# Folded weights of four batches made at once on two row halves of TensorE, kept in DRAM

## Chip, cores and metric

The kernel runs on one core of one Trainium2 chip. The metric is device time in microseconds of one execution, taken as the median of several runs. The engines are named as in the profile: PE is TensorE (PEld its weight loads), DVE is VectorE, ACT is ScalarE, POOL is GpSimd, SP is SyncE. SP and POOL issue nearly all DMAs here, each from a queue of its own that is worked off in order.

## What is computed

Memory attention followed by a two-layer network without biases, all in float32:

```python
a   = softmax(phi, over the 576 tokens)          # phi: 8 batches, 8 heads, 576 tokens, 32 memories
k_m = einsum('bhsm,bhsd->bhmd', a, k)            # 32 x 64 for each batch and head
v_m = einsum('bhsm,bhsd->bhmd', a, v)
attn = softmax(q @ k_m.T / 8)                    # 576 x 32
x   = (attn @ v_m), heads side by side           # 4608 tokens x 512
out = relu(x @ w_in)**2 @ w_out                  # w_in 512 x 2048, w_out 2048 x 512
```

The kernel never forms x. It folds v_m into w_in: for each batch, VW = v_m @ w_in (for each head 32 x 64 times 64 x 2048), so that x @ w_in = attn @ VW. This folding is what the change is about.

## The kernel before

**Numbers.** Full precision is kept by splitting each operand into a high part that the fast float32r matmul takes exactly and a low part, and by three products: high*high, high*low, low*high.

**Stages.** The 8 batches are worked off one after the other (0 and 1 interleaved by halves). For each batch there are 16 steps, one for each 128 columns of w_in. A step has `mm1` (line 822): 12 matmuls, attention weights times folded weights, 6 for 256 tokens and 6 for 320, then on ACT and DVE relu, square and the split into `gh` and `glo`; and `mm2` (line 857): 12 matmuls of 512 columns that add to four accumulator banks. `mm2_left` (line 891) does the last 64 tokens of two batches together, 48 matmuls.

**What feeds a batch.** `memory(b, hh)` (line 481) makes k_m and v_m for four heads: a maximum over tokens (`mx`), exp, a sum (`asum`), then 20 float32 matmuls (line 526) that use the array as four column strips of 32, so that four heads are worked side by side; then `kT` for the scores and, through `values` (line 591), the stationary operand `VT` of the folding. `attention(b)` (line 793) makes the attention weights. `vw_step(n, s, hh)` (line 632) does the folding for a pair of batches, 2n and 2n+1: one slice s of 256 columns and one half hh of the chunks. It has 6 matmuls of 256 columns with a block-diagonal stationary operand (128 rows are two heads of 64, the columns are two heads of two batches, and half of the entries are zero), then for each half of the partitions one copy on ACT (line 340, called from 647) and one subtraction on DVE (line 648). A pair takes 16 such steps, and before each, `wi_again` (line 448) loads 512 KB of the prepared w_in from a DRAM copy, `w_in_kept`.

**Buffers.** `V0` to `V7` hold the folded weights of the second batch of a pair, `vw0` (two buffers) those of the first. `mx` is one buffer, used for `mx` and `asum` in turn. `KV` is one buffer, `wi` has three. In PSUM there are four banks `acc`, two banks `h`, one bank `pv` (folding) and one bank `pa` (memory and scores).

**Order.** Nothing is scheduled by hand. `Plan` (line 57) takes all operations with estimated costs, simulates a list schedule forward, then backward (from which due times follow), tries several leads for the operations marked `lead`, and keeps the order whose modelled end is earliest. The order for each engine is fixed in the program; engines meet by semaphores. The last pairs of the program:

```python
    for n in range(1, NPAIR):
        ...
        for b in (b0, b1):
            for hh in (0, 1):
                memory(b, hh)
        attention(b0)
        for s in range(NSL):
            vw_alloc(n, s)
            for hh in (0, 1):
                wi_again(n, s, hh)
                vw_step(n, s, hh)
        ...
        attention(b1)
```

Of the kernel before, what the change touches and what calls it, by code (L numbers as in the profile page):

```python
# [19 lines left out]
P = 128  # L20
# [36 lines left out]
class Plan:  # L57
# [59 lines left out]
    def order(self):  # L117
        for o in reversed(self.ops):
            e = next(iter(o.ways))
            cost = min(o.ways.values()) + (SEES[e] if o.lat is None else o.lat)  # L120
            if o.size:
                cost += sum(n / r for n, r in o.size) + FIRST[e] + LANDS[e] + 300
            late = min((u.late for u in o.users), default=1e9)
            if o.cap is not None:
                late = min(late, o.cap)
            o.late = late - cost
        keys = [o.late - (LEAD if o.lead else 0) for o in self.ops]
        best = self.forward(keys), keys
# [12 lines left out]
        return out  # L141
# [8 lines left out]
    def forward(self, keys):  # L150
# [27 lines left out]
        while left:  # L178
# [35 lines left out]
            for u in o.users:  # L214
                u.count -= 1
                u.ready = max(u.ready, o.end + self.slack(o, u, e))
                if not u.count:
                    add(u)
        return max(o.end for o in self.ops)

    def backward(self):
# [17 lines left out]
        for _ in self.ops:  # L239
# [18 lines left out]
            for x in o.deps:  # L258
                x.ready = max(x.ready, t + self.slack(x, o, x.left) + (0 if x.size else self.seen(x, x.left)))
# [27 lines left out]
def tile_attention_moe(  # L287
# [92 lines left out]
    kept = dram.tile([NSL * 2 * P, 4 * SL], F32, name="w_in_kept")  # L380
    w_kept = plan.buf("w_in_kept", lambda _: kept)
    wi = {}
    wo = {}
# [78 lines left out]
    def vt_alloc(n):  # L462
        for i in (0, 1) if n == 0 else (1 - n % 2,):
            t = [st([P, 4, P], F32R, f"VT{x}{i}", f"VT{x}{n}{i}") for x in "hl"]
            if n:
                VT[2 * n] = VT[2 * n + 1] = t
                continue
# [13 lines left out]
    def memory(b, hh, where=None):  # L481
# [32 lines left out]
        pk = bank(f"pkv{u}")  # L514
        rot = 2 * (b % 2)

# [16 lines left out]
        def sums(e):  # L533
            if asum is None:
                for c in range(SC):
                    r = P if c < NMAIN else LEFT
                    for s in range(4):
                        nc.tensor.matmul(pk()[32 * s:32 * s + 32, 2 * D:2 * D + 1], a()[0:r, (s + rot) % 4, c, :], ones[0:r],
                                         start=(c == 0), stop=(c == SC - 1), tile_position=(0, 32 * s))
            elif b % 2 == 0:  # L540
                nc.tensor.matmul(pk()[:, 2 * D:2 * D + 1], asum(), ones, start=True, stop=True)
# [6 lines left out]
        if b < 2:  # L548
            for i in (0, 1):
                op({"PE": 800}, lambda e, i=i: mm(e, i), [A, KV[i], (pk, "sum")], [(pk, i)], lead=True, lat=120)  # L550
        else:
            op({"PE": 1400}, lambda e: mm(e, 0), [A, KV[0], KV[1], (pk, "sum")], [(pk, 0), (pk, 1)], lead=True, lat=120)
        rs = st([P, 1], F32, "rs", f"rs{u}")
# [4 lines left out]
        if b < 2:  # L558
# [32 lines left out]
    def values(b, hh, pv, at):  # L591
        vh, vl = VT[b]
        for s in (0, 1):
            ch = 2 * hh + ((s + b) % 2)
# [17 lines left out]
    def vw_alone(s, bp):  # L612
# [11 lines left out]
        for hh in (0, 1):  # L624
            op({"PE": 712}, lambda e, hh=hh: mm(e, hh), [ts_[hh], vh, vl], [pw], lead=True)
        V = VW[bp, s]
# [5 lines left out]
    def vw_step(n, s, hh):  # L632
# [8 lines left out]

        op({"PE": 712}, mm, [t, vh, vl], [pw], lead=True)
        for hf in (0, 1):
# [6 lines left out]


    att = {}

    def scores(b, hh, split):

        u = f"{b}_{hh}"
        Q = st([P, NC * D], F32, "q", f"q{u}")
        for x in (0, 1):
            h0 = 4 * hh + 2 * ((x + b) % 2)
            dma(lambda d, x=x, h0=h0: d(Q()[64 * x:64 * x + 64], q[b, h0:h0 + 2].rearrange("h (p c) d -> (h p) (c d)", c=NC)),  # L660
# [333 lines left out]
    for g in range(24, 32):  # L994
        step(g)
    for n in range(1, NPAIR):
        b0, b1 = 2 * n, 2 * n + 1
        vt_alloc(n)
        for b in (b0, b1):
            for hh in (0, 1):  # L1000
                memory(b, hh)
        attention(b0)
        for s in range(NSL):
            vw_alloc(n, s)
            for hh in (0, 1):
                wi_again(n, s, hh)
                vw_step(n, s, hh)
            for ff in (2 * s, 2 * s + 1):
                step(pos[b0, ff])
        attention(b1)  # L1010
        for ff in range(NFF):
            step(pos[b1, ff])

# [33 lines left out]
```

## Time and profile before

| | |
|---|---|
| median of 3 runs | 774.26 us (772.9 to 774.47) |
| the profiled execution, its own time | 774.0 us |
| its span, first to last instruction | 772.1 us |
| PE busy | 749.8 us (97%) |
| DVE busy | 562.0 us (73%) |
| ACT busy | 364.6 us (47%) |
| DMA | 101.54 MB, mean 132 GB/s |

A busy time is the union of the spans of an engine's instructions. Matmuls are pipelined: one of 512 columns is shown with some 400 ns, yet the next one starts 230 ns later. What a matmul costs is therefore read from start to start in the timeline, not from its duration.

### The profile page before, as it was taken

To read this page: it belongs to the slowest core of one execution; us is meant where nothing else is said; L and a number is where in the kernel's file an instruction comes from. 1 tells how busy PE (TensorE), PEld (TensorE's weight loads), DVE (VectorE), ACT (ScalarE), POOL (GpSimd) and SP (SyncE) were. 2 spreads that over 40 slices of the span, in tenths; PEclk is the share of its full clock that TensorE was granted. 3 is DMA by queue.
4 is the path that set the end of the run, shared out by engine and by line. 5 is a ranking of instruction groups with operands and counts; after the bars stand their busy time and mean duration, and the time that the engine had idled before them with its cause. 6 is when DMAs were issued, how large, how long until landed. Compare 5 with 4: busy or idle time off the path is not lost.

```text
span 772.1 us, 13135 instructions
## 1 busy us (share of the span) xinstructions
PE 749.8 (97%) x4998; PEld 646.3 (84%) x4998; DVE 562.0 (73%) x1164; ACT 364.6 (47%) x782; POOL 54.5 (7%) x95
## 2 busy tenths in 40 slices
PE   5889999999999999999999999999999999999997
PEld 3667888888888888888788888888888888888886
DVE  4999999997579655758779567966779566874451
ACT  2767689775443555442333444433335344532330
POOL 4111212111000000010001100010000100000000
PEclk9999999999999999999999999999999999999999
DMA  9998878578556332223545434222334432100002
GB/s 275 338 273 226 263 248 229 172 229 232 155 145 210 102 101 91 59 56 85 147 109 156 134 105 123 81 56 68 93 87 128 129 115 85 31 25 31 1 1 68
DMA packets 70046, 101.54 MB, mean 132 GB/s; under 512 B 21792, under 2 KB 48416, under 8 KB 69984
## 3 DMA queue, kind: packets, MB, share of 16 engines
q1 hardware_dynamic: 59392, 81.41, 35.7%
q0 software_dynamic: 10496, 19.17, 9.3%
q8 instruction: 39, 0.64, 0.4%
q10 hardware_dynamic: 96, 0.13, 0.1%
q14 instruction: 23, 0.19, 0.1%
HBM read 79.17 MB, written 17.83 MB: 126 GB/s over the span
## 4 chain that ended last, share of the span: by engine, by line
PE 83%; DVE 10%; ACT 3%; issue 2%; DMA 1%; SPq 0%; DVEq 0%; ACTq 0%
PE h L843 23%; PE acc L876 14%; PE acc L873 14%; PE acc L874 14%; PE accl L899 6%; PE pvw L640 5%; PE psc L677 3%; PE pkv L526 3%; DVE work L409 1%; DVE work L424 1%; DVE mx L504 1%; DVE vw L648 1%; DVE work L406 1%; DVE wi L439 1%; DVE glo L853 1%
## 5 line engine op out<-in xcount | busy, mean ns | idle before, releaser
L843 PE MATMUL h<-ath,vw 128*128 128x320 f32 (+1 forms) x1024 | 208.1, 298 | 0.2 <-ACT r L847 0.2
L873 PE MATMUL acc<-wo,gh 128*128 128x512 f32 x512 | 206.6, 403 | 0.0
L874 PE MATMUL acc<-wo,gh 128*128 128x512 f32 x512 | 201.9, 394 | 0.0
L843 PEld LDWEIGHTS h<-ath,vw 128*128 128x128 f32 x1024 | 170.7, 189 | 14.3 <-ACT r L847 0.6
L876 PE MATMUL acc<-wo,glo 128*128 128x512 f32 x512 | 158.8, 404 | 0.0
L849 ACT ACTIVATE gh<-r 128x512 fp32r<-128x512 f32 x128 | 81.0, 633 | 110.3 <-DVE r L848 106.3
L340 ACT CAST vw<-pvw 64x512 fp32r<-64x512 f32 (+1 forms) x128 | 74.4, 581 | 99.8 <-PE pvw L640 70.3
L873 PEld LDWEIGHTS acc<-wo,gh 128*128 128x128 f32 x512 | 96.7, 189 | 18.2 <-issue 0.4
L843 PE MATMUL h<-atl,vw 128*128 128x256 f32 (+1 forms) x512 | 110.0, 296 | 0.9 <-DVE atl L778 0.5
L874 PEld LDWEIGHTS acc<-wo,gh 128*128 128x128 f32 x512 | 96.7, 189 | 16.3
L876 PEld LDWEIGHTS acc<-wo,glo 128*128 128x128 f32 x512 | 92.0, 189 | 17.4 <-issue 1.6
L648 DVE TENSOR_TENSOR vw<-pvw,vw 64x512 fp32r<-64x512 f32 x112 | 77.1, 688 | 38.3 <-ACT vw L340 36.5
L853 DVE TENSOR_TENSOR glo<-r,gh 128x512 fp32r<-128x512 f32 x128 | 87.7, 685 | 8.7 <-ACT r L851 5.9
L847 ACT ACTIVATE r<-h 128x256 f32<-128x256 f32 (+1 forms) x151 | 60.6, 411 | 69.6 <-PE h L843 66.8
L848 DVE TENSOR_SCALAR r<-h 128x320 f32<-128x320 f32 (+1 forms) x105 | 47.9, 456 | 56.2 <-PE h L843 55.1
L843 PEld LDWEIGHTS h<-atl,vw 128*128 128x128 f32 x512 | 82.5, 189 | 1.4 <-DVE atl L778 0.7
L852 DVE TENSOR_TENSOR r<-r 128x576 f32<-128x576 f32 x59 | 44.7, 758 | 30.7 <-ACT gl L850 28.2
L899 PE MATMUL accl<-wo,gl 128*128 128x512 f32 x192 | 53.8, 396 | 0.0
L851 ACT ACTIVATE r<-r 128x576 f32<-128x576 f32 x69 | 47.3, 685 | 1.8
L640 PE MATMUL pvw<-wi,VTh 128*128 128x256 f32 x224 | 42.4, 282 | 1.2 <-DVE vw L648 1.2
L640 PEld LDWEIGHTS pvw<-wi,VTh 128*128 128x128 f32 x224 | 37.2, 188 | 6.1 <-issue 1.9
L899 PEld LDWEIGHTS accl<-wo,gl 128*128 128x128 f32 x192 | 34.8, 188 | 6.8
(143 smaller groups left out, 799.6 us busy)
## 6 DMA issues: line engine op xcount, KB each, us to landing
wi<-w_in_kept SPq DMA_DIRECT2D x56, 512.0 KB
KV<-in_v_dram SPq DMA_DIRECT2D x16, 512.0 KB
KV<-in_k_dram SPq DMA_DIRECT2D x16, 512.0 KB
raw<-in_moe_w_in_dram SPq DMA_DIRECT2D x16, 512.0 KB
raw<-in_moe_w_out_dram SPq DMA_DIRECT2D x16, 512.0 KB
w_in_kept<-wi POOLq DMA_DIRECT2D x16, 512.0 KB, 4.6
q<-in_q_dram SPq DMA_DIRECT2D x24, 288.0 KB
out_dram<-o POOLq DMA_DIRECT2D x20, 256.0 KB, 7.8
```

What stands on the lines that cost most here:

```text
L340: nc.scalar.copy(o, i) if e == "ACT" else ENG[e].tensor_copy(o, i)
L640: nc.tensor.matmul(pw()[:, x * SL:(x + 1) * SL], l()[:, 2 * x + hh, :], t()[:, r, x, :], start=(i == 0), stop=(i == 2))
L648: vec({"DVE": 700}, lambda e, part=part, pr=pr: nc.vector.tensor_sub(part(1), pw()[pr], part(0).bitcast(F32)), [pw, (V, (0, hf))], [(V, (1 ...
L843: nc.tensor.matmul(p()[:, 0:n], V()[:, l, hh, c0:c0 + P], x()[:, hh, cs], start=(i == 0), stop=(i == 5))
L847: op({"ACT": act(n) - 40, **({} if b < 2 else {"DVE": tt(n)})}, lambda e, cs=cs, n=n, p=p: nc.scalar.activation(r()[:, cs], p()[:, 0:n], A ...
L848: else nc.vector.tensor_scalar(r()[:, cs], p()[:, 0:n], 0.0, None, ALU.max), [p], [(r, h)])
L849: op({"ACT": act(SM)}, lambda e: nc.scalar.activation(gh(), r()[:, 0:SM], AF.Square), [r], [gh])
L853: vec({"DVE": tt(SM)}, lambda e: nc.vector.tensor_sub(glo(), r()[:, 0:SM], gh().bitcast(F32)), [r, gh], [glo])
L873: nc.tensor.matmul(a(), gh()[:, c], t()[:, 0], start=f0, stop=False)
L874: nc.tensor.matmul(a(), gh()[:, c], t()[:, 1], start=False, stop=False)
L876: nc.tensor.matmul(a(), glo()[:, c], t()[:, 0], start=False, stop=f1)
L899: nc.tensor.matmul(a(), G()[:, l, :], t()[:, w], start=(ff == 0 and n == 0), stop=(ff == NFF - 1 and n == 2))
```

## The change

**Four batches at once.** For batches 4 to 7 `vw_step` is replaced by `vw_quad(s, hh)`. The 128 rows of a w_in chunk are two heads of 64. The stationary operand now holds for the rows of one head the 32 memories of all four batches as 128 columns, with no zeros. Each former matmul over 128 rows becomes two over 64 rows, on the upper and the lower half of the array, into two PSUM banks (`pv` and `pa`). There are 16 such steps of 12 matmuls instead of 32 steps of 6.

**Through DRAM.** The result (a head's slice for four batches on 128 partitions) is split in a tile `fold` (in the room of `KV`), stored to a DRAM tensor by POOL (two stores of 512 KB for each step) and loaded by slice and batch with four DMAs of 128 KB each on SP (`vw_again`) into `V0` to `V7`.

**Order of the program.** All four batches need their v_m first, so `memory` of batches 4 to 7 moves into the steps of batch 2. The k_m of batches 5 to 7 (`kT`) is made in the buffer `mx`, stored to DRAM by POOL and loaded again by SP ahead of the scores. The folding steps stand among the steps of batches 3 and 4: `WHEN` is (2, 5, 8, 11, 14) and (1, 4, 7), and `quad(s)` is `wi_again` and `vw_quad` for both hh. Batches 5 and 7 use the form of the sums that even batches have (line 541, in place of 544).

**Planner.** It takes two matmul operations that follow each other on PE as free of latency, counts 730 for `vw_step` (was 712), 1560 for the memory matmuls (was 1400), 900 for `vw_quad`, and makes more trials.

```diff
-        for _ in range(2):
+        for _ in range(4):
...
-            for lead in (0, 3000, 9000):
+            for lead in (0, 1500, 3000, 6000, 9000):
...
-                u.ready = max(u.ready, o.end + self.slack(o, u, e))
+                u.ready = max(u.ready, t + d if e == "PE" and "PE" in u.ways else o.end + self.slack(o, u, e))
...
+    folded = dram.tile([NSL * 4 * P, 4 * SL], F32, name="vw_kept")
+    w_folded = plan.buf("vw_kept", lambda _: folded)
+    keys = dram.tile([6 * P, 2 * M], F32, name="kT_kept")
+    QUAD = B - 4
...
-        kT = kTs[b, hh] = st([P, 2, 1, M], F32, f"kT{b % 2}{hh}", f"kT{u}")
+        kT = st([P, 2, 1, M], F32, f"kT{b % 2}{hh}" if b <= QUAD else "mx", f"kT{u}")
...
+        if b <= QUAD:
+            kTs[b, hh] = kT
+        else:
+            at = 2 * (b - QUAD - 1) + hh
+            dma(lambda d: d(keys[at * P:(at + 1) * P], kT().rearrange("p u o m -> p (u o m)")), [(2 * M * P * 4, 256)],
+                r=[kT], w=[(w_keys, at)], eng="POOL", lead=True)
...
+    def vw_quad(s, hh):
...
+        Z = room[0]
+        t = wi[QUAD // 2, s, 1, hh]
+        vh, vl = VT[QUAD]
+        pw = [pt(x, f"pvq{s}_{hh}_{x}") for x in ("pv", "pa")]
...
+            for x in (0, 1):
+                for i, (l, r) in enumerate(((vh, 0), (vh, 1), (vl, 0))):
+                    for g in (0, 1):
+                        rows = slice(64 * g, 64 * g + 64)
+                        nc.tensor.matmul(pw[g]()[:, x * SL:(x + 1) * SL], l()[rows, 2 * x + hh, :], t()[rows, r, x, :],
+                                         start=(i == 0), stop=(i == 2), tile_position=(64 * g, 0))
+        op({"PE": 900}, mm, [t, vh, vl], pw, lead=True)
+        for g in (0, 1):
+            part = lambda l, g=g: Z()[:, g, l].rearrange("p x f -> p (x f)")
+            op({"ACT": acp(2 * SL)}, lambda e, part=part, g=g: copy(e, part(0), pw[g]()), [pw[g]], [(Z, (g, 0))], lead=True)
+            vec({"DVE": tt(2 * SL)}, lambda e, part=part, g=g: nc.vector.tensor_sub(part(1), pw[g](), part(0).bitcast(F32)),
+                [pw[g], (Z, (g, 0))], [(Z, (g, 1))], lead=True)
+            at = 4 * s + 2 * hh + g
+            dma(lambda d, g=g, at=at: d(w_folded()[at * P:(at + 1) * P, :], Z()[:, g].rearrange("p l x f -> p (l x f)").bitcast(F32)), [(4096 * P, 4096)],
+                r=[(Z, (g, 0)), (Z, (g, 1))], w=[(w_folded, at)], eng="POOL", lead=True)
...
+    def vw_again(b, s):
+        V = VW[b, s] = st([P, 2, 2, SL], F32R, f"V{s}", f"vw{b}_{s}")
+        for h in range(4):
+            at = (4 * s + h) * P + 32 * (b - QUAD)
+            dma(lambda d, h=h, at=at: d(V()[32 * h:32 * h + 32].rearrange("p l x f -> p (l x f)").bitcast(F32), w_folded()[at:at + 32, :]), [(4096 * 32, 4096)],
+                issue=440, r=[(w_folded, 4 * s + h)], w=[(V, h)], lead=True)
...
+    for s in range(NSL):
+        vw_alloc(1, s)
+        for hh in (0, 1):
+            wi_again(1, s, hh)
+            vw_step(1, s, hh)
+        for ff in (2 * s, 2 * s + 1):
+            step(pos[2, ff])
+        if s == 0:
+            vt_alloc(2)
+        if s == 3:
+            attention(3)
+        memory(QUAD + s // 2, s % 2)
+    for ff in range(NFF):
+        step(pos[3, ff])
+        if ff in WHEN[0]:
+            quad(WHEN[0].index(ff))
+        if ff == 9:
+            attention(4)
+    for b in range(QUAD, B):
+        for ff in range(NFF):
+            if ff % 2 == 0:
+                vw_again(b, ff // 2)
+            step(pos[b, ff])
+            if b == QUAD and ff in WHEN[1]:
+                quad(len(WHEN[0]) + WHEN[1].index(ff))
+            if ff == 9 and b + 1 < B:
+                attention(b + 1)
```

## Rows read from the trace of the kernel before

**Rows 1.** The windows view: PE, PEld, DVE, ACT and POOL busy us with their instruction counts, the granted clock, the DMA share and GB/s; first the stretches of the start, then from 180 us those of the batches (243 is the start of batch 2, then 3, 4, 5, 6, 7; 757 is the tail).

```profile
20.00:60.00 40.00, 34.71 (x411) 27.16 (x410) 37.38 (x88) 27.46 (x57) 5.15 (x10) 0.96 1.03 300
...
140.00:180.00 40.00, 38.81 (x222) 33.58 (x221) 37.18 (x73) 29.53 (x62) 5.34 (x8) 1.00 0.75 219
...
243.00:326.00 83.00, 83.00 (x476) 73.70 (x475) 55.88 (x109) 42.92 (x89) 1.63 (x3) 1.00 0.34 104
326.00:422.00 96.00, 95.28 (x652) 80.98 (x651) 70.48 (x153) 35.05 (x79) 4.97 (x10) 1.00 0.42 106
422.00:508.00 86.00, 86.00 (x490) 76.12 (x489) 61.88 (x123) 38.01 (x78) 2.70 (x4) 1.00 0.34 105
508.00:598.00 90.00, 90.00 (x630) 76.79 (x629) 66.91 (x144) 34.95 (x79) 4.57 (x9) 1.00 0.36 92
598.00:686.00 88.00, 88.00 (x498) 77.82 (x497) 61.54 (x120) 39.29 (x82) 2.58 (x4) 1.00 0.26 79
686.00:757.00 71.00, 71.00 (x392) 62.67 (x391) 35.91 (x70) 19.97 (x49) 0.00 (x0) 1.00 0.05 16
```

**Rows 2.** The timeline of PE around one folding step (start us, us, engine, line, tiles, shape, count).

```profile
480.22 0.40 PE L640 MATMUL pvw<-wi,VTh 128*128 128x256 f32 x2
...
480.57 0.40 PE L640 MATMUL pvw<-wi,VTh 128*128 128x256 f32 x2
...
480.93 0.39 PE L873 MATMUL acc<-wo,gh 128*128 128x512 f32 x1
481.16 0.39 PE L874 MATMUL acc<-wo,gh 128*128 128x512 f32 x1
```

**Rows 3.** The groups by line and form: the folding of the pairs on PE, ACT and DVE (busy us, mean ns of one, idle before).

```profile
L640 PE MATMUL pvw<-wi,VTh 128*128 128x256 f32 x224 | 42.4, 282 | 1.2 <-DVE vw L648 1.2
L340 ACT CAST vw<-pvw 64x512 fp32r<-64x512 f32 x112 | 65.0, 580 | 97.2 <-PE pvw L640 70.3 <-PE h L843 25.4 <-DVE vw L648 0.5
L648 DVE TENSOR_TENSOR vw<-pvw,vw 64x512 fp32r<-64x512 f32 x112 | 77.1, 688 | 38.3 <-ACT vw L340 36.5
L853 DVE TENSOR_TENSOR glo<-r,gh 128x512 fp32r<-128x512 f32 x128 | 87.7, 685 | 8.7 <-ACT r L851 5.9
```

**Rows 4.** The timeline of PE around the memory matmuls on column strips (L526, a row merges 40) and the sums of an even batch (L541).

```profile
543.45 0.39 PE L874 MATMUL acc<-wo,gh 128*128 128x512 f32 x1
543.68 0.28 PE L541 MATMUL pkv<-ones,asum 128*128 128x1 f32 x2
543.82 0.48 PE L873 MATMUL acc<-wo,gh 128*128 128x512 f32 x1
544.13 0.40 PE L874 MATMUL acc<-wo,gh 128*128 128x512 f32 x1
544.46 1.43 PE L526 MATMUL pkv<-KV,phi 128*32 128x128 f32 x40
545.82 0.50 PE L873 MATMUL acc<-wo,gh 128*128 128x512 f32 x1
546.15 0.40 PE L874 MATMUL acc<-wo,gh 128*128 128x512 f32 x1
```

**Rows 5.** From the chain of work that ended last: four full-array float32 matmuls of 320 columns (psc), and the strip matmuls.

```profile
567.29 1.36 PE pkv L526 x40
...
576.00 1.08 PE psc L677 x4
```

**Rows 6.** The timeline of PEld (weight loads) around the same place.

```profile
543.79 0.19 PEld L873 LDWEIGHTS acc<-wo,gh 128*128 128x128 f32 x1
543.90 0.19 PEld L874 LDWEIGHTS acc<-wo,gh 128*128 128x128 f32 x1
```

**Rows 7.** The timeline of PE around the sums of an odd batch (L544).

```profile
555.23 0.40 PE L874 MATMUL acc<-wo,gh 128*128 128x512 f32 x1
555.56 0.28 PE L544 MATMUL pkv<-ones,asum 128*64 128x1 f32 x4
555.77 0.50 PE L876 MATMUL acc<-wo,glo 128*128 128x512 f32 x1
556.20 0.65 PE L526 MATMUL pkv<-KV,phi 128*32 128x128 f32 x16
```

**Rows 8.** The timeline of DVE: two units of `memory` among the steps.

```profile
532.03 1.33 DVE L504 TENSOR_REDUCE mx<-phi 128x128 f32<-128x640 f32 x1
...
539.96 0.81 DVE L510 TENSOR_TENSOR phi<-phi,pmx 128x640 f32<-128x640 f32 x1
...
541.93 1.34 DVE L531 TENSOR_REDUCE asum<-phi 128x128 f32<-128x640 f32 x1 [0.42 <-ACT phi L512]
...
544.17 1.33 DVE L504 TENSOR_REDUCE mx<-phi 128x128 f32<-128x640 f32 x1
...
546.53 0.24 DVE L582 STREAM_TRANSPOSE kT<-kvn 128x64 f32<-128x64 f32 x1
```

**Rows 9.** DMA issues: queue, count, KB each, and where shown the median us from issue to landing.

```profile
w_in_kept<-wi POOLq DMA_DIRECT2D x16, 512.0 KB, 4.6
...
out_dram<-ol POOLq DMA_DIRECT2D x6, 128.0 KB, 6.7
```

**Rows 10.** The timeline of SP's queue: two issues one behind the other (start us, us).

```profile
535.43 0.61 SPq L459 DMA_DIRECT2D KV<-in_v_dram  x1
536.08 0.62 SPq L460 DMA_DIRECT2D KV<-in_v_dram  x1
```

More of the change, by code (lines that the diff above doesn't have):

```diff
@@ L258, in backward @@
             for x in o.deps:
-                x.ready = max(x.ready, t + self.slack(x, o, x.left) + (0 if x.size else self.seen(x, x.left)))
+                x.ready = max(x.ready, t if x.left == o.left == "PE" else t + self.slack(x, o, x.left) + (0 if x.size else self.seen(x, x.left)))
                 x.count -= 1
@@ L381, in tile_attention_moe @@
     w_kept = plan.buf("w_in_kept", lambda _: kept)
+    folded = dram.tile([NSL * 4 * P, 4 * SL], F32, name="vw_kept")
+    w_folded = plan.buf("vw_kept", lambda _: folded)
+    keys = dram.tile([6 * P, 2 * M], F32, name="kT_kept")
+    w_keys = plan.buf("kT_kept", lambda _: keys)
+    QUAD = B - 4
     wi = {}
@@ L465, in vt_alloc @@
             if n:
-                VT[2 * n] = VT[2 * n + 1] = t
+                for b in range(2 * n, B if 2 * n == QUAD else 2 * n + 2):
+                    VT[b] = t
                 continue
@@ L514, in memory @@
         pk = bank(f"pkv{u}")
-        rot = 2 * (b % 2)
+        odd = b % 2 if b < QUAD else 0
+        rot = 2 * odd
         def mm(e, which):
@@ L539, in sums @@
                                          start=(c == 0), stop=(c == SC - 1), tile_position=(0, 32 * s))
-            elif b % 2 == 0:
+            elif odd == 0:
                 nc.tensor.matmul(pk()[:, 2 * D:2 * D + 1], asum(), ones, start=True, stop=True)
@@ L551, in memory @@
         else:
-            op({"PE": 1400}, lambda e: mm(e, 0), [A, KV[0], KV[1], (pk, "sum")], [(pk, 0), (pk, 1)], lead=True, lat=120)
+            op({"PE": 1560}, lambda e: mm(e, 0), [A, KV[0], KV[1], (pk, "sum")], [(pk, 0), (pk, 1)], lead=True, lat=120)
         rs = st([P, 1], F32, "rs", f"rs{u}")
@@ L592, in values @@
         vh, vl = VT[b]
+        if b >= QUAD:
+            i = b - QUAD
+            for r in (0, 1):
+                rows = slice(64 * r, 64 * r + 64)
+                src = lambda rows=rows, r=r: pv()[rows, at:at + P].rearrange("p (g x m) -> p g x m", g=2, x=2)[:, :, r, :]
+                to = lambda t, rows=rows: t()[rows, 2 * hh:2 * hh + 2, 32 * i:32 * i + 32]
+                op({"ACT": acp(64), "DVE": tt(64)}, lambda e, src=src, to=to: copy(e, to(vh), src()), [pv], [(vh, (b, hh, r))], lead=True)
+                vec({"DVE": tt(64)}, lambda e, src=src, to=to: nc.vector.tensor_sub(to(vl), src(), to(vh).bitcast(F32)),
+                    [pv, (vh, (b, hh, r))], [(vl, (b, hh, r))], lead=True)
+            return
         for s in (0, 1):
@@ L624, in vw_alone @@
         for hh in (0, 1):
-            op({"PE": 712}, lambda e, hh=hh: mm(e, hh), [ts_[hh], vh, vl], [pw], lead=True)
+            op({"PE": 730}, lambda e, hh=hh: mm(e, hh), [ts_[hh], vh, vl], [pw], lead=True)
         V = VW[bp, s]
@@ L649, in vw_step, with mm @@
                 [pw, (V, (0, hf))], [(V, (1, hf))], lead=True, lat=30)
+    room = []
+    WHEN = (2, 5, 8, 11, 14), (1, 4, 7)
+    def vw_quad(s, hh):
+        if not room:
+            room.append(st([P, 2, 2, 2, SL], F32R, "KV", "fold"))
+        Z = room[0]
+        t = wi[QUAD // 2, s, 1, hh]
+        vh, vl = VT[QUAD]
+        pw = [pt(x, f"pvq{s}_{hh}_{x}") for x in ("pv", "pa")]
+        def mm(e):
+            for x in (0, 1):
[19 more added lines that the diff above has]
+                issue=440, r=[(w_folded, 4 * s + h)], w=[(V, h)], lead=True)
     att = {}
@@ L656, in scores @@
         u = f"{b}_{hh}"
+        if b > QUAD:
+            kT = kTs[b, hh] = st([P, 2, 1, M], F32, f"kT{b % 2}{hh}", f"kTa{u}")
+            at = 2 * (b - QUAD - 1) + hh
+            dma(lambda d: d(kT().rearrange("p u o m -> p (u o m)"), keys[at * P:(at + 1) * P]), [(2 * M * P * 4, 256)],
+                r=[(w_keys, at)], w=[kT], lead=True)
         Q = st([P, NC * D], F32, "q", f"q{u}")
         for x in (0, 1):
-            h0 = 4 * hh + 2 * ((x + b) % 2)
+            h0 = 4 * hh + 2 * ((x + (b if b < QUAD else 0)) % 2)
             dma(lambda d, x=x, h0=h0: d(Q()[64 * x:64 * x + 64], q[b, h0:h0 + 2].rearrange("h (p c) d -> (h p) (c d)", c=NC)),
@@ L995, in tile_attention_moe, with quad @@
         step(g)
[L996 to L1010, printed above, removed]
-        for ff in range(NFF):
-            step(pos[b1, ff])
+    vt_alloc(1)
+    for b in (2, 3):
+        for hh in (0, 1):
+            memory(b, hh)
+    attention(2)
+    def quad(s):
+        for hh in (0, 1):
+            wi_again(QUAD // 2, s, hh)
+            vw_quad(s, hh)
+    for s in range(NSL):
+        vw_alloc(1, s)
+        for hh in (0, 1):
+            wi_again(1, s, hh)
[14 more added lines that the diff above has]
+    for b in range(QUAD, B):
+        for ff in range(NFF):
+            if ff % 2 == 0:
[5 more added lines that the diff above has]
+                attention(b + 1)
     with tc.manual_schedule():
```

2 lines of the change are left out of this document (1 added, 1 removed).

## The prediction, on record before the change ran

> **What bounds the kernel now.** I read the windows first, cut at the batches. From 243 us to 757 us PE's busy time is the whole of each stretch (83.00 of 83, 86.00 of 86, 90.00 of 90, 88.00 of 88, 71.00 of 71; one stretch lacks 0.7), at a granted clock of 1.00, the upper of its two levels (2.4 GHz), while DVE is busy 51 to 74% and the DMA engines 5 to 42% [rows 1]. Before 180 us it is different: from 20 to 60 us and from 140 to 180 us DVE is busy 93% and PE has holes of 5.3 and 1.2 us [rows 1]. So for two thirds of the span the time is the sum of what PE issues, and an operation taken off PE there is worth its whole issue time, wherever it stood. Busy time alone doesn't prove this, since a pipelined matmul of 512 columns is shown with 0.39 us though the next starts after 0.23. So next comes the timeline, from start to start: six folding matmuls start at 480.22 and the next operation at 480.93, which is 0.71 us or 0.118 each [rows 2]. PE issues without a hole; it is the bound, and the price list below is made of starts.
>
> The sum is made against the profiled execution, 774.0 us (span 772.1 and 1.9 around it). The median of the runs, 774.26, lies 0.3 above, less than I can resolve. A difference under about 0.2% (1.5 us) can't be told from none.
>
> **Part 1, folding steps removed.** Batches 4 to 7 had 2 pairs x 16 steps = 32 steps. 32 x 0.71 = 22.7 us [rows 2], all on the path, since PE is full in both stretches where they lie (422 to 508 and 598 to 686) [rows 1]. Their 64 copies on ACT at 0.58 and 64 subtractions on DVE at 0.69 go too [rows 3]; 32 and 32 over 128 partitions come instead, at nearly the same 0.59 and 0.685 (the DVE figure is that of another 128x512 subtraction) [rows 3]. This takes some 22 us off DVE and 18 off ACT, worth nothing by itself, as neither is the bound there.
>
> **Part 2, the four-batch step.** 16 steps of 12 matmuls, six pairs, each pair on the two row halves of the array. No row of this kernel shows row halves at work. The nearest are the column strips of `memory`: 40 matmuls of 128 columns take 1.36 us [rows 4, 5]. Four full-array float32 matmuls of 320 columns take 1.08 [rows 5], 0.27 each and 0.84 ns a column, so 128 columns would take 0.108 alone and forty in a row 4.3 us. At 1.36 four strips do run side by side: ten groups of 0.108 are 1.08, and 0.28 is left over. The left-over is the change of shape: one inside (from 128 to 64 rows) and one at the end, 0.14 each. Ahead of the strips the last full matmul takes 544.13 to 544.46, 0.33 instead of 0.23, so 0.10 more; behind them the first takes 545.82 to 546.15, again 0.10 more [rows 4]. By these rows a folding step on halves costs six pairs at 0.118 = 0.71, plus 0.10 + 0.14 + 0.10 = 1.05 us. Lower end: 0.71, if changing between halves and whole costs nothing. Upper end: the halves wait for each other, 12 x 0.118 + 0.34 = 1.76. I take 1.0, near the strip rows, a little less because part of the 0.14 is the slow first group of the 64-row run. 16 x 1.0 = 16.0 us, ends 11.4 and 28.2.
>
> One thing keeps the upper end alive. Full weight loads of 128 columns that nothing covers start 0.11 us apart (543.79 and 543.90) [rows 6]. A half needs all 128 columns of its weights, so a pair needs two loads: 0.22 if they go one behind the other, 0.11 if side by side. Four strip loads of 32 columns in 0.108 fit both readings. The Trainium skill, "TensorE: Matmul & The Clock Gate", has a rule on each side: its section "LDWEIGHTS (loading the stationary operand)" says that a load's time goes by its columns and not by its rows (estimate from its P / 1.2: 107 ns for 128 columns, and the trace agrees with 0.11), which speaks against splitting rows; its Part 3 says that loads overlap running matmuls where the row group differs, and gives for two tiles the time of one and some 4 ns, by which a step would be 6 x 0.122 = 0.73 and the sum 4 us lower than mine. No run here shows it for halves.
>
> **Part 3, sums of batches 5 and 7.** Four units change from the odd to the even form. Odd: 0.10 ahead (555.23 to 555.56 against 0.23), 0.21 itself, 0.10 behind (555.77 to 556.20 is 0.43; 0.10 of the excess belongs to the strips that follow) = 0.41 [rows 7]. Even: 0.14 itself and 0.08 behind (543.82 to 544.13) = 0.22 [rows 4]. 4 x 0.19 = 0.8 us off PE.
>
> **Part 4, transfers.** Out: 16 loads of 512 KB of w_in. In: 32 stores of 512 KB, 128 loads of 128 KB, 6 + 6 small ones of `kT`. Net some 25 MB between 326 and 757 us, 58 GB/s on top of 16 to 106, where the start moves 300 [rows 1]: hidden. SP issues four loads for each slice at 0.62 us [rows 10], 2.5 us in the 9 us of two steps. A slice's buffer is free after two steps of the batch before and needed 14 steps later. A late load would stop PE, whose order is fixed; the cover is those 60 us. Cost 0. On POOL the stores stand in one queue with the output stores; nothing on PE waits for them directly.
>
> **Part 5, `memory` moved into batch 2.** PE's work is the same wherever it stands. DVE's isn't: batch 2 has 55.9 us of DVE work in 83 [rows 1]. Eight units come in at about 5.5 us (3.5 us of it in three rows, `mx` 1.33, `asum` 1.34 and the subtraction 0.81 [rows 8]; 2 estimated for a dozen small ones): some 100 us of DVE work in a stretch that grows by the strips to about 100. Against this, relu and squares can go to ACT, which is busy 42.9 of 83 [rows 1], and a unit may slip into batch 3, which loses its four units. There is also a new wait. So far the next unit's `mx` starts before this unit's `kT` (544.17 and 546.53) [rows 8]; now `kT` of batches 5 to 7 sits in the buffer `mx` and must be stored by POOL first, 4.6 to 6.7 us from issue to landing [rows 9]. Queued behind a waiting `mx` on DVE is the subtraction `glo`, for which PE's second layer waits. Six units, each between 0 and 1 us through to PE: 0 to 6 us. I take 0.5 in all, since the plan has 14 us for a unit (532.03 to 546.53) [rows 8] and can put other DVE work ahead.
>
> **Part 6, planner.** The order changes everywhere, the start included, where 5.3 and 1.2 us of holes lie [rows 1]. It can gain or lose there, from -3 to +3; I take 0. With a full PE another order of the same matmuls gains nothing later.
>
> **Sum:** 774.0 - 22.7 + 16.0 - 0.8 + 0.5 = 767.0 us.
>
> **Rivals.**
> - *The halves don't overlap* (the change then doesn't do what it says). With loads one behind the other a step costs 12 x 0.11 + 0.34 = 1.66, sixteen 26.6: 774.0 - 22.7 + 26.6 - 0.8 + 0.5 = 777.6; with the matmuls too, 1.76 each: 779. It decides from (22.7 + 0.3) / 16 = 1.44 us a step upward. For it: two full loads a pair [rows 6], and no row with halves. Against it: strips do run four at a time [rows 4, 5]. Chance 0.08, and slower.
> - *DVE becomes the bound of batch 2*, or its wait for the stored `kT` reaches PE. At the start, with DVE at 93%, PE lacks 1.2 in 40 us and more [rows 1]; over 100 us that is 3, with the wait up to 6 more: 770 to 776. For it: the 100 us of work in 100. Against: ACT has room and the units can slip. Chance 0.13.
> - *The halves cost no change of shape, or the new order closes holes at the start*: step 0.71 to 0.9, 761 to 765. Chance 0.17.
>
> **How the numbers follow.** Forecast 767.0 with 0.62, its own range 765 to 769.5. To hold 8 in 10 the range takes the better case down to 762 and the DVE case up to 773; beyond it stay the overlap rival, the dear end of the DVE case and the cheapest of the third. Faster than 772.7: 0.62 + 0.17 + 0.08 = 0.87, less 0.01 for a bad order at the start, 0.86. Within 0.2%: 0.04 from the DVE case and 0.01, 0.05. Slower: 0.08 and the DVE case's end 0.01, 0.09.
>
> **What would show it.** In the profile after: 192 matmuls of 64 rows, the two of a pair a few ns apart, pairs 0.118 apart, and 0.9 to 1.05 us from the first of a step to the next full matmul (overlap rival: 0.22 and 1.5 or more). PE busy in every window from batch 2 on, each batch shorter by its folding alone; fewer DVE microseconds in batches 4 to 7, more in batch 2. Wrong for the DVE case would be: holes in PE in batch 2 released by DVE, with DVE waiting for the DMA of `kT`. PE holes at the start of batches 4 to 7 released by a DMA would mean that Part 4's cover failed.

## The result and the profile after

The changed kernel takes 780.57 us (median of 4 runs, 780.05 to 783.23), the kernel before 773.58 on the same chip: ratio 1.0099, 95% interval 1.007 to 1.0129. It is slower by 7 us where 7 us faster was forecast. The profiled execution of after took 780.05 us (span 778.3), that of before 774.0 (772.1).

The head of the page of after, then the shares of its chain and two of its DMA groups:

```profile
PE 746.3 (96%) x4990; PEld 634.1 (81%) x4990; DVE 539.7 (69%) x1121; ACT 346.5 (45%) x761; POOL 78.0 (10%) x133
...
PE 74%; DVE 14%; issue 6%; DMA 3%; ACT 2%; SPq 1%; POOL 0%; DVEq 0%; POOLq 0%; ACTq 0%
...
vw_kept<-fold POOLq DMA_DIRECT2D x32, 512.0 KB, 4.1
vw<-vw_kept SPq DMA_DIRECT2D x128, 128.0 KB
```

PE is busy 3.5 us less than before (749.8), and yet the span is 6.2 longer: PE stood idle 32.0 us instead of 22.3. The windows view (columns as in [rows 1]) says where. Before, cut at other places than in [rows 1]:

```profile
0.00:180.00 180.00, 163.00 (x1356) 137.78 (x1357) 161.15 (x344) 125.27 (x264) 33.39 (x55) 0.98 0.84 251
180.00:380.00 200.00, 199.46 (x1341) 171.63 (x1341) 138.56 (x293) 92.06 (x200) 9.68 (x21) 1.00 0.44 122
380.00:760.00 380.00, 379.66 (x2272) 330.95 (x2271) 260.87 (x526) 147.30 (x319) 11.41 (x19) 1.00 0.29 82
```

After:

```profile
0.00:180.00 180.00, 159.35 (x1332) 134.27 (x1333) 159.16 (x339) 123.20 (x259) 36.24 (x55) 0.99 0.84 243
180.00:380.00 200.00, 193.08 (x1471) 160.19 (x1469) 151.57 (x330) 94.48 (x204) 14.69 (x32) 1.00 0.61 169
380.00:760.00 380.00, 380.00 (x2131) 328.66 (x2130) 226.01 (x448) 128.19 (x298) 27.11 (x46) 1.00 0.43 127
```

Length less PE busy is PE's idle time. From 0 to 180 us it grew from 17.0 to 20.65, in a stretch of which the diff changes no operation. From 180 to 380, where `memory` of batches 4 to 7 now stands, it grew from 0.5 to 6.9. From 380 to 760 PE is full, though all loads of the stored weights lie there: in after the transfers (Part 4) cost nothing. The granted clock (third column from the end) is 1.00 from 180 us on in both traces, and 0.98 in before and 0.99 in after ahead of it: the lower of TensorE's two levels (1.2 GHz) is no part of the loss between these two traces.

**The four-batch step** (timeline of PE in after):

```profile
453.71 0.40 PE L910 MATMUL h<-ath,vw 128*128 128x256 f32 x2
454.03 0.38 PE L692 MATMUL pvq_pv<-wi,VTh 64*128 64x256 f32 x1
454.04 0.38 PE L692 MATMUL pvq_pa<-wi,VTh 64*128 64x256 f32 x1
454.26 0.28 PE L692 MATMUL pvq_pv<-wi,VTh 64*128 64x256 f32 x1
454.26 0.28 PE L692 MATMUL pvq_pa<-wi,VTh 64*128 64x256 f32 x1
454.38 0.28 PE L692 MATMUL pvq_pv<-wi,VTl 64*128 64x256 f32 x1
...
454.73 0.28 PE L692 MATMUL pvq_pv<-wi,VTl 64*128 64x256 f32 x1
...
454.94 0.50 PE L943 MATMUL acc<-wo,glo 128*128 128x512 f32 x1
455.28 0.86 PE L966 MATMUL accl<-wo,gl 128*128 128x512 f32 x3
```

The two of a pair start within 0.01 us and pairs 0.12 apart, the pace of full matmuls [rows 2]: the halves do run side by side, loads included. The change of shape has its price: 0.08 ahead (the row of 453.71 holds two matmuls of 0.12, so the step could start at 453.95), 0.23 instead of 0.12 for the first pair, 0.21 instead of 0.12 from the last pair to 454.94, and then 0.34 instead of 0.23 for the first full matmul. That is 1.10 us for a step, of which 0.71 is work and 0.39 shape.

**The wait in 180 to 380 us.** The waits view of PE from 180 to 400 us in after (line, what it waited for; us, times, longest):

```profile
PE pvt L601 <- DVE vx L597: 1.8, 3, 0.9
PE pmx L512 <- DVE mx L510: 1.8, 3, 0.8
PE pvt L601 <- DVE kT L589: 1.3, 2, 0.7
```

And its chain of waits in order of time (start, us, what):

```profile
325.95 3.08 DMA kT_kept<-kT
...
330.48 1.32 DVE mx L510
...
331.94 0.30 PE pmx L512
...
357.14 4.87 DMA kT_kept<-kT
...
362.08 1.30 DVE mx L510
...
363.53 0.30 PE pmx L512
```

PE stops at the small transposes inside `memory`. In the chain, the maximum `mx` starts 1.5 and 0.1 us after the store of the last unit's `kT` out of the same buffer has landed, which was 3.08 and 4.87 us after its issue (the six such stores took 1.8 to 5.7 us, median 4.6), and soon PE stands at the transpose of `mx`. Of the 6.9 us, 1.8 are read at that transpose and 3.1 at later transposes of the units.

### The profile page after: what moved, and what is told of

It reads as the page before. It is cut to its first block, busy times and chain, and to the rows that moved or that the text cites. A ratio compares the mean times of both kernels' runs of the same rounds, so it can differ in the third digit from the quotient of the medians.

```text
span 778.3 us, 13334 instructions
## 1 busy us (share of the span) xinstructions
PE 746.3 (96%) x4990; PEld 634.1 (81%) x4990; DVE 539.7 (69%) x1121; ACT 346.5 (45%) x761; POOL 78.0 (10%) x133
## 4 chain that ended last, share of the span: by engine, by line
PE 74%; DVE 14%; issue 6%; DMA 3%; ACT 2%; SPq 1%; POOL 0%; DVEq 0%; POOLq 0%; ACTq 0%
PE h L910 21%; PE acc L943 12%; PE acc L940 12%; PE acc L941 12%; PE accl L966 6%; PE psc L744 3%; PE pkv L533 2%; PE pvq_pv L692 2%; DVE work L414 2%; PE pvw L663 1%; DVE work L429 1%; DMA KV<-in_k_dram 1%; DMA KV<-in_v_dram 1%; DVE vw L671 1%; DVE mx L510 1%
## 5 line engine op out<-in xcount | busy, mean ns | idle before, releaser
L910 PE MATMUL h<-atl,vw 128*128 128x320 f32 (+1 forms) x512 | 109.8, 296 | 0.0
L914 ACT ACTIVATE r<-h 128x320 f32<-128x320 f32 (+1 forms) x170 | 68.7, 411 | 81.6 <-PE h L910 80.2
L915 DVE TENSOR_SCALAR r<-h 128x320 f32<-128x320 f32 (+1 forms) x86 | 39.0, 453 | 82.7 <-PE h L910 82.2
L919 DVE TENSOR_TENSOR r<-r 128x576 f32<-128x576 f32 x73 | 55.3, 757 | 44.2 <-ACT gl L917 42.1
L966 PE MATMUL accl<-wo,gl 128*128 128x512 f32 x192 | 48.1, 396 | 0.0
L340 ACT CAST vw<-pvw 64x512 fp32r<-64x512 f32 (+1 forms) x64 | 37.2, 581 | 18.6 <-PE pvw L663 16.4
L918 ACT ACTIVATE r<-r 128x576 f32<-128x576 f32 x55 | 37.7, 686 | 1.4
L671 DVE TENSOR_TENSOR vw<-pvw,vw 64x512 fp32r<-64x512 f32 x48 | 32.9, 685 | 1.3 <-ACT vw L340 0.2
L917 ACT ACTIVATE gl<-r 128x64 fp32r<-128x64 f32 x128 | 30.9, 241 | 0.0
L533 PE MATMUL pkv<-KV,phi 128*32 128x128 f32 (+3 forms) x800 | 26.8, 273 | 3.1 <-issue 1.8
```

Source lines behind the costliest of these rows:

```text
L533: nc.tensor.matmul(pk()[32 * s:32 * s + 32, o], a()[0:r, h, c, :], src, start=(c == 0), stop=(c == SC - 1), tile_position=(0, 32 * s))
L671: vec({"DVE": 700}, lambda e, part=part, pr=pr: nc.vector.tensor_sub(part(1), pw()[pr], part(0).bitcast(F32)), [pw, (V, (0, hf))], [(V, (1 ...
L910: nc.tensor.matmul(p()[:, 0:n], V()[:, l, hh, c0:c0 + P], x()[:, hh, cs], start=(i == 0), stop=(i == 5))
L914: op({"ACT": act(n) - 40, **({} if b < 2 else {"DVE": tt(n)})}, lambda e, cs=cs, n=n, p=p: nc.scalar.activation(r()[:, cs], p()[:, 0:n], A ...
L915: else nc.vector.tensor_scalar(r()[:, cs], p()[:, 0:n], 0.0, None, ALU.max), [p], [(r, h)])
L919: else nc.vector.tensor_mul(r(), r(), r()), [r], [r])
```

## Experiments

Two theories after the first reading. *Order*: `Plan` lays the whole program anew, and the new order of the start, with holes of its own, costs what the folding saves. *Wait*: `mx` on the stored `kT` reaches PE. A third one came up later, *density*: eight memory units inside batch 2 are too many small DVE steps. And against all of them stands the thought that the *shape change* costs more than the timeline shows. Times are medians; "ratio" is to the kernel before on the same chip, with its 95% interval behind it, and differences between two kernels are those of their ratios, at 774 us. "Idle" is PE's, from 0 to 180 / 180 to 380 / 380 to 540 us, from the windows of the profiled run (before 17.0 / 0.5 / 0.3, after 20.65 / 6.9 / 0). It counts holes alone: time in which PE works at the lower clock is busy time, so the granted clock has to be read beside it. What it is worth can be seen in the kernel before, whose 84 runs beside the experiments have a median of 772.8 us at a mean clock of 1.000 (30 runs) and of 774.4 us at 0.996 or less (15 runs).

**1. The planner alone.** `plan_only` is the kernel before with the planner's part of the diff (rule, trials, the counts 730 and 1560); `old_plan` is after with the old rule and trials:

```diff
-        for _ in range(4):
+        for _ in range(2):
...
-            for lead in (0, 1500, 3000, 6000, 9000):
+            for lead in (0, 3000, 9000):
...
-                u.ready = max(u.ready, t + d if e == "PE" and "PE" in u.ways else o.end + self.slack(o, u, e))
+                u.ready = max(u.ready, o.end + self.slack(o, u, e))
```

> The kernel before with the planner's part of the change alone (no latency between two matmul operations, more trials, 1560 for the memory matmuls, 730 for the folding steps); no folding on halves, no DRAM, memory where it was. Theory 1 (the new planning rules give a worse order): 3 us or more above the kernel before, with more PE holes before 180 us and at the transposes of the memory units. Theory 2 (the moved memory units and the buffer mx): within 2 us of the kernel before. Theory 3 (any new order of this program costs or gains some us at the start, whatever the change): a shift of 2 to 4 us, nearly all of it before 180 us.

> The changed kernel with the old planning rules and the old trials; its costs, folding on halves and moved memory stay. Theory 1 (planning rules): 768 to 771, close to the forecast, PE's holes at the memory transposes gone. Theory 2 (moved memory units and the buffer mx): within 2 us of the changed kernel (780.6), with mx still waiting for the stored kT. Theory 3: a shift of 2 to 4 us before 180 us, either way.

`plan_only`: 786.38 us, ratio 1.0163 (1.0144 to 1.0182). The same operations as before, on a PE said to be full, 12.6 us slower. Windows of it:

```profile
0.00:180.00 180.00, 156.52 (x1319) 132.28 (x1320) 156.83 (x335) 123.36 (x259) 34.68 (x55) 0.98 0.82 242
180.00:380.00 200.00, 197.93 (x1296) 170.30 (x1297) 139.40 (x291) 90.29 (x196) 9.47 (x20) 1.00 0.45 126
```

Idle 23.5 / 2.1 / 2.2: the start alone lost 6.5 us in holes. `old_plan`: 780.36, 1.0087 (1.0068 to 1.0107), idle 21.6 / 2.2 / 0. So the rule is not simply at fault: with the old one the start loses as much and the total stays.

**2. Another buffer for the stored `kT`.** `kt_in_qT` is after, `kt_in_qT_old_plan` is `old_plan`, each with

```diff
-        kT = st([P, 2, 1, M], F32, f"kT{b % 2}{hh}" if b <= QUAD else "mx", f"kT{u}")
+        kT = st([P, 2, 1, M], F32, f"kT{b % 2}{hh}" if b <= QUAD else "qT", f"kT{u}")
```

> The changed kernel, where kT of batches 5 to 7 waits for its store in the buffer qT (used by the scores alone) and no longer in mx. All else stays. Theory 2a (the wait of mx for the stored kT is the cost): 773 to 776; the steps from DMA kT_kept to mx are gone from the chain, and PE's holes at the transposes of mx with them. Theory 2b (eight memory units in one batch are the cost, because PE waits in order for their small DVE steps): 1 to 2 us faster at most, PE still waits at the transpose of vx. Theory 1: within 2 us of the changed kernel.

> Both: kT in qT and the old planning rules. If the planning rules and the wait of mx each cost their part and add up: 765 to 769. If the eight units in one batch are the cost (theory 2b): 777 or more.

795.6 us (1.0276, 1.0256 to 1.0296; idle 24.4 / 10.3 / 7.15) and 775.16 (1.0017, 1.0005 to 1.003; idle 17.8 / 7.1 / 0). One edit, 13.7 us worse under one planner and 5.4 better under the other. The edit re-plans everything too, so it tells nothing by itself: where it gained, the holes of the start shrank (21.6 to 17.8), which the edit doesn't touch, and those of 180 to 380 us grew (2.2 to 7.1); and `qT` isn't free, since the scores of another batch then wait for the store. That called for an edit that leaves the start alone.

**3. Start held.** The engine and place of all that the kernel before's plan starts ahead of 235 us are written into the program; the counts and the old rule and trials are before's, the rest is planned freely:

```diff
+        keys = [self.pins[i][1] if i in self.pins else k for i, k in enumerate(keys)]
...
-            for e in o.ways:
+            for e in (self.pins[o.seq][0],) if o.seq in self.pins else o.ways:
```

`pin_after` is after with this. `pin_kvn` in addition swaps two buffers for batches 5 to 7, so that `mx` waits for `kvn` (which is soon done with) and not for the store:

```diff
-        kvn = st([P, D], F32, "kvn", f"kvn{u}")
+        kvn = st([P, D], F32, "kvn" if b <= QUAD else "mx", f"kvn{u}")
...
-        kT = st([P, 2, 1, M], F32, f"kT{b % 2}{hh}" if b <= QUAD else "mx", f"kT{u}")
+        kT = st([P, 2, 1, M], F32, f"kT{b % 2}{hh}" if b <= QUAD else "kvn", f"kT{u}")
```

> The changed kernel with the old planning rules and costs, where each operation that the kernel before starts ahead of 235 us in its plan keeps the engine and the place that it has there (a list of times in the program; the first 1339 operations come out in the same order as in the kernel before). Folding on halves, moved memory units, kT in mx stay. Theory 3 (a good part of the loss is the new order of the start, which the change doesn't touch): PE holes before 180 us are back at those of the kernel before (36.9 us), 772 to 775. If the start's order is worth nothing: 779 to 782, as old_plan.

> As pin_after, but for batches 5 to 7 the buffers are exchanged: kvn lies in mx and kT in the buffer of kvn, so that no operation waits for the store of kT but the next kT some 12 us later. Theory 2a (the wait of mx for the stored kT costs PE time): 2 to 4 us below pin_after, PE's holes at the transpose of mx in batch 2 gone. Theory 2b (PE waits in order for late small DVE steps, since eight units lie in one batch): within 1 us of pin_after, holes at the transposes of vx and mx still there.

`pin_after`: 775.43 us, 1.0023 (1.0012 to 1.0034), idle 16.7 / 3.5 / 3.1. (Its expectation gives 36.9 us of holes before 180 us for the kernel before; the windows give 17.0.) `pin_kvn`: **770.56 us, 0.9958 (0.9938 to 0.9978)**, idle 17.2 / 1.1 / 0.4, faster than both kernels. Windows of `pin_kvn`:

```profile
0.00:180.00 180.00, 162.82 (x1374) 136.79 (x1378) 161.37 (x346) 126.75 (x267) 35.08 (x55) 1.00 0.86 252
180.00:380.00 200.00, 198.94 (x1518) 166.69 (x1511) 155.02 (x334) 94.35 (x210) 16.83 (x36) 1.00 0.63 180
...
sum 765.20, PE 742.04 PEld 632.33 DVE 535.50 ACT 346.67 POOL 76.98; mean PE 185.51 PEld 158.08 DVE 133.88 ACT 86.67 POOL 19.24
```

5.0 us from `old_plan` to `pin_after` (the held start, with before's counts; its holes shrink by 4.9), 5.0 from there to `pin_kvn` (the swap). PE's waits for `mx` from 180 to 400 us, 1.8 in after, are 1.6 in `pin_after` and none in `pin_kvn`. That is less than 5.0: the swap, too, gives a new order behind the start, and 2.6 us of the holes that it closed lie from 380 to 540 us, where no `mx` waits.

**4. Density.** `pin_move45` is before, start held, with nothing of the change but `attention(3)` and `memory` of batches 4 and 5 moved into the steps of batch 2. `pin_kvn_margin` is `pin_kvn` with 800 instead of 250 ns of room ahead of PE where the order is free:

```diff
+                if s in (0, 1):
+                    memory(4, s)
+                if s in (4, 5):
+                    memory(5, s - 4)
...
-        return 600 if o.size else MARGIN if "PE" in u.ways and e != "PE" else 0
+        return 600 if o.size else (MARGIN if u.seq in self.pins else 800) if "PE" in u.ways and e != "PE" else 0
```

> The kernel before, same held start, where alone the memory units of batches 4 and 5 and attention of batch 3 move into the steps of batch 2 (no folding on halves, nothing through DRAM). Theory 2b: the move alone costs 1.5 to 3 us, 775.5 to 777. Rival (moving costs nothing, PE's work is the same wherever it stands, as forecast): 773 to 775.

> As pin_kvn, but the plan leaves 800 ns instead of 250 between the end of another engine's work and the matmul that needs it, for all operations that are not held at the place of the kernel before. Theory 2b: PE finds these results ready, its holes between 240 and 400 us shrink by 2 to 4 us, 2 to 4 us below pin_kvn. Rival (the memory chain itself is too slow for batch 2, whatever the order): the holes stay or grow, 0 to 4 us above pin_kvn.

774.83 us (1.0011, 0.9998 to 1.0023; idle 17.0 / 0 / 0) and 771.52 (0.9969, 0.9954 to 0.9983; idle 17.05 / 0 / 3.25). Moving half of the units costs at most 0.23%. Room ahead of PE empties 180 to 380 us of holes and gives them back a stretch later. And `pin_kvn` has all eight units in batch 2, with 1.1 us of holes from 180 to 380 us. Density is not the main cause.

**5. The price of a shape change.** `pin_kvn_split` has the order of `pin_kvn` and puts one full-array matmul of one column, whose result is overwritten, into the middle of each four-batch step, so that PE changes shape twice more:

```diff
         def mm(e):
             for x in (0, 1):
+                if x:
+                    nc.tensor.matmul(pw[0]()[:, SL:SL + 1], ident, ones, start=True, stop=True)
```

> As pin_kvn (same order of all operations on all engines), but in the middle of each folding step on halves stands one more matmul on the whole array (128 rows, one float32 column, its result overwritten). Each of the 16 steps thus changes shape twice more. If a change of shape costs what the trace shows (0.38 us for both ends of a step) and PE is the bound there, 16 x (0.38 + 0.14 for the matmul) = 8.3 us above pin_kvn. If changes of shape are hidden: 16 x 0.14 to 0.22 = 2.2 to 3.5 us above.

777.28 us, 1.0045 (1.0031 to 1.0059): 6.7 us more than `pin_kvn`, 0.42 for each of the 16. Its timeline of PE:

```profile
486.96 0.38 PE L779 MATMUL pvq_pv<-wi,VTh 64*128 64x256 f32 x1
...
487.30 0.28 PE L779 MATMUL pvq_pa<-wi,VTl 64*128 64x256 f32 x1
487.51 0.38 PE L775 MATMUL pvq_pv<-ones,ident 128*128 128x1 f32 x2
487.82 0.38 PE L779 MATMUL pvq_pv<-wi,VTh 64*128 64x256 f32 x1
...
488.36 0.50 PE L1027 MATMUL acc<-wo,gh 128*128 128x512 f32 x1
```

1.40 us from the first of the step to the full matmul behind it, against 0.91 in after: 0.49 on the timeline, of which the small matmul itself is a part. The intervals leave some 2 us either way around the 6.7. Within that it agrees with the 8.3 expected for a change of shape that is paid in full; that the change costs more than the timeline shows is not borne out.

**6. Rule, trials and the swap, each without the other.** `pin_kvn_rule` and `pin_kvn_trials` give the free part of `pin_kvn` the new rule or the new trials; `kt_in_kvn` is `old_plan` with the swap, nothing held.

> As pin_kvn, but with the new planning rule (no latency between two matmul operations) for all operations that are not held at the place of the kernel before. Theory 1 (the rule itself makes worse orders, by letting PE wait in order for other engines): 3 us or more above pin_kvn, more PE holes between 235 and 520 us. Theory 3 (it is the order of the start that was lost): within 1.5 us of pin_kvn.

> As pin_kvn with the old rule, but with the changed kernel's number of trials (four times five leads). Another order of the same program after 235 us. Theory 3 and a bound of PE: within 1.5 us of pin_kvn. If orders with the same modelled work differ by several us even behind the start, 773 or more.

> As pin_kvn, but no operation is held at a place of the kernel before (old rules, the changed kernel's costs 730 and 1560): the start is planned anew. Theory 3: slower than pin_kvn by what the new start loses, 3 to 8 us, with PE's holes before 180 us above 20 us in sum against 17 in the kernel before. If the start's order is worth nothing: within 1 us of pin_kvn.

771.84 us (0.9977, 0.9963 to 0.9992), 772.93 (0.9991, 0.9975 to 1.0007), 776.27 (1.0039, 1.0014 to 1.0063). Behind a held start the rule costs 1.5 and the trials 2.6, and the intervals still overlap with that of `pin_kvn`. Letting the start go (with after's counts) costs 6.3. Not all of that lies in the start: its holes grow by 3.8, to 21.0, and the profiled run of `kt_in_kvn` (781.91 us, the slowest of ten) also stands 4.0 us at one four-batch step, in this window, where the mean granted clock falls to 0.84:

```profile
440.00:460.00 20.00, 16.03 (x77) 13.36 (x77) 6.67 (x13) 3.86 (x8) 1.87 (x3) 0.84 0.77 226
```

**7. From after itself.** After with its own rule and trials, and the start held with before's counts (`held_start`), the two buffers swapped (`free_mx`), and both (`held_free`).

> The changed kernel with its own planning rule and trials; the operations that the kernel before starts ahead of 235 us in its plan are held at their place there, with the old costs 712 and 1400. kT stays in mx. If the start's order is worth its holes: PE idle before 180 us back from 20.7 to 17 us, 3 to 5 us below the changed kernel, 775 to 777. If not: 779 to 782.

> The changed kernel, nothing held, where for batches 5 to 7 kvn lies in mx and kT in the buffer of kvn: the wait of mx for the stored kT is gone, all else is planned anew by the new rules. If the wait of mx is worth 5 us under any order: 774 to 777. If the newly planned start decides: anywhere from 772 to 790, and PE's idle time before 180 us differs from the changed kernel's 20.7 by most of the difference.

> Both: start held and mx freed, under the new rule and trials. If the two causes are all of the loss: 769 to 773, 8 to 11 us below the changed kernel. If the new rule or the four-batch steps cost more by themselves: 775 or more.

778.34 us (1.0057, 1.0037 to 1.0077; idle 17.3 / 5.3 / 2.7), 784.95 (1.0141, 1.0117 to 1.0165; idle 19.7 / 7.0 / 4.7), 773.25 (0.999, 0.9974 to 1.0007; idle 17.5 / 4.3 / 0.6). Both undone give back 8.4 us, from 1.0099 to 0.999: the whole loss against the kernel before, but not the 7 us that were forecast below it. The swap is worth 5.2 us behind a held start; with the start let go it makes the kernel 3.3 slower than after. Neither expectation for `free_mx` fits: it is slower than after, and yet its start has somewhat fewer holes (19.7 against 20.65). The timeline shows why it lost:

```profile
468.80 0.59 ACT L340 CAST fold<-pvq_pv 128x512 fp32r<-128x512 f32 x1 [5.70 <-DMA vw_kept<-fold]
...
470.21 0.55 PE L692 MATMUL pvq_pv<-wi,VTh 64*128 64x256 f32 x1 [4.69 <-issue]
```

Here ACT waits 5.70 us until the store has left the one buffer `fold`, and the next four-batch step stands on PE for 4.69. The step then takes 1.58 us to the next full matmul instead of 0.91, at a mean granted clock of 0.83 from 460 to 480 us. The free order had put two steps too close. After itself has no such hole; `kt_in_qT` has one of 6.10, behind a wait of 7.30, and `kt_in_kvn` the one of 4.0, behind a wait of 4.41. Nor do the holes from 180 to 380 us follow the wait of `mx` alone: with it they are 2.2 us (`old_plan`) to 6.9 (after), and without it, the start let go, 2.5 (`kt_in_kvn`), 7.0 (`free_mx`), 7.1 and 10.3 (the two with `kT` in `qT`), where PE waits mostly for other steps of `memory`.

## Why the prediction was wrong

**Part 6 failed first.** It took 0 for the new order, with -3 to +3, because "with a full PE another order of the same matmuls gains nothing later". It allowed a loss of 3 at the start and none behind it, and forgot that another order can lose anywhere. PE is full only in the order that was found for before. In the runs here the four-batch program alone came out between 770.56 and 795.6 us with orders that differ by nothing but rule, counts, held places and the buffers of `kT` and `kvn`, and before's own program lost 12.6 with the planner's part. The start, whose operations the change does not touch, has 3.65 us more of holes in after; holding it, with before's counts, was worth 3.3 (`held_start`) and 5.0 (`pin_after`), and its holes shrank by 3.3 and 4.9. The 6.3 (`pin_kvn` against `kt_in_kvn`) and 11.7 (`held_free` against `free_mx`) are more than the start: its holes differ by 3.8 and 2.1 there, and both free orders stand at a four-batch step.

**Part 5 failed too.** The mechanism was named rightly: `mx` waits for the landing of `kT`, which came in 1.8 to 5.7 us (median 4.6) where 4.6 to 6.7 was read [rows 9]. It was mis-sized: 0.5 taken, while the edit that takes the wait away was worth 5.0 and 5.2 behind a held start, near the upper end of 6. PE's rows show 1.6 and 1.9 us of this directly (`pin_after`, `held_start`, at the transpose of `mx`). That the rest is the same wait is not shown: the edit lays the order behind the start anew, and with the start let go it left as many holes from 180 to 380 us (`free_mx` 7.0, after 6.9). Part 5 is short by 1 us at least, and by up to 5. The prediction looked at what is queued behind `mx` on DVE. It didn't look at what is queued behind the transpose of `mx` on PE, which issues in order as well: the waits that the profile shows are at the transposes L512 and L601, not at PE's second layer behind `glo`. Its own sign for the DVE case, holes of PE in batch 2 released by DVE, is in the trace. The "14 us for a unit" that were to cover it are the length of one unit in before's order, from its `mx` to its `kT`; the next `mx` came 12.1 us behind the first there [rows 8], and neither tells the new order's.

**The other terms of the sum stood, but for 1.6 us.** Part 2's mechanism was right and its size nearly: 1.10 us a step on the timeline where 1.0 was taken and 1.05 derived from the strips; 16 x 0.10 = 1.6 us. The overlap rival is refuted. Beside the row, the rule of the Trainium skill ("TensorE: Matmul & The Clock Gate", Part 3), time of one and some 4 ns for two tiles, agrees with pairs 0.12 us apart; the step of 0.73 worked out from it left out the change of shape, 0.39 here. To see Parts 1 to 3 together, before and `pin_kvn` are cut in two where both have started the same matmuls in the same held order (229.22 and 227.10 us):

```profile
0.00:229.22 229.22, 212.06 (x1755) 178.31 (x1756) 194.20 (x420) 149.97 (x319) 36.42 (x63) 0.99 0.80 234
229.22:772.10 542.88, 537.78 (x3244) 467.97 (x3242) 367.77 (x745) 214.67 (x463) 18.07 (x32) 1.00 0.31 88
```

```profile
0.00:227.10 227.10, 209.92 (x1756) 176.00 (x1756) 193.97 (x420) 149.72 (x319) 38.09 (x63) 1.00 0.81 236
227.10:765.20 538.10, 532.12 (x3236) 456.33 (x3234) 341.53 (x696) 196.95 (x448) 38.89 (x70) 1.00 0.47 137
```

Behind the cut PE busy is 5.7 us less. Parts 1 to 3 gave 22.7 - 16.0 + 0.8 = 7.5, and with the measured step of 1.10 they give 5.9. The stretch is 4.8 us shorter, near the 3.3 of all runs' ratio. The other 2.1 us by which this one span of `pin_kvn` is shorter were gained ahead of the cut, by the same matmuls in the same order; in before's trace the granted clock was 0.94 from 40 to 100 us, in that of `pin_kvn` 1.00, and its 768.12 us is among the shorter of its runs (767.85 to 772.52). That part is luck of the execution.

From the forecast to the measured ratio it is 14.7 us. The two edits of `held_free` give back 8.4, the step was 1.6 dearer, and `pin_kvn`, with the old rule and trials, lies 2.5 below `held_free`; the last 2.2 are not found, and are of the size of the intervals.

**Transfers.** Part 4 held in after, but not in every order: "nothing on PE waits for them directly" left out the one buffer `fold`, through which `free_mx`, `kt_in_qT` and `kt_in_kvn` do.

**The chances.** Slower had 0.09, made of the overlap rival and the dear end of the DVE case; a bad order at the start had 0.01, and that counted as no change. DVE as the bound of batch 2 ended at 776 with the wait already inside; the result is that wait and a bad order together, which no case had.

**What stays open.** Which property of a new start makes it lose is not settled; the places of its longest waits differ from order to order (in after PE waits 3.3 us once for `kvx`, L570; in before 2.5 in two waits for `vw`). How the 6.4 us by which after's holes grew in 180 to 380 us divide between `mx`'s wait and the rest of the chain can't be read off either, since each edit re-plans what follows. The held runs take before's counts (712 and 1400) along with before's start, and no run changes the counts alone, so what is put to the held start is that of both. Why the granted clock fell in the start of some executions and not of others with the same held order (before and `pin_kvn`) is open too. Two buffers `fold` were not tried.

## What to carry to other kernels

Where a program's order is computed, an edit is two changes: the operations and the order of everything. Price the second from the spread of orders, not as 0, measure an edit with the order of the untouched part held, and lay the granted clock beside busy time, which counts slow work in full. A full PE is full in one order only; ask of each in-order engine, PE too, what stands behind an instruction that waits. A buffer that a store must leave before its next use makes the engine that writes it next wait: stores of 32 KB landed 1.8 to 5.7 us after their issue here, and ACT waited up to 7.30 us for `fold`.

## What the runs showed of the hardware

- Two 64-row matmuls with 128-column weights run side by side at the rate of one, loads included: behind the first pair of a step, pairs of 256 columns start 0.12 us apart, as full ones did [rows 2].
- Going from the whole array to halves and back costs 0.39 us a visit: 0.08 ahead, 0.11 in the first pair, 0.09 behind the last and 0.11 in the first full matmul. A second visit inside a step cost 0.42 by the times of `pin_kvn_split`, the small matmul included (0.49 on its timeline).
- PE busy is no fixed sum of the same matmuls, since slow time counts in full. With 4990 matmuls each it is 742.0 to 743.9 us in the four profiles with a mean granted clock of 0.999 or more (`pin_kvn`, `held_free`, `kt_in_qT_old_plan`, `pin_kvn_rule`), and 750.5 and 750.1 in the two with the lowest, `free_mx` (0.989) and `kt_in_qT` (0.986).
- In the 20 us around a hole of 4.0, 4.69 or 6.10 us on an otherwise full PE (`kt_in_kvn`, `free_mx`, `kt_in_qT`) the mean granted clock is 0.84, 0.83 and 0.83, where it is 1.00 in the same stretch of after; the four-batch step right behind the hole took 1.58 us in `free_mx` instead of 0.91.
